# Waits for a burst's loads of q, keys and score rows, moved to the last product of the run in front

## The chip, the cores and the metric

The kernel runs on one core of a Trainium2 chip. The metric is the device time of one execution in microseconds; less is better. The kernel before takes 1772.36 us (median of 3 runs, 1772.31 to 1773.91).

## The reference, cut to what matters

Two attentions over one input x of 2048 rows and 512 columns, 32 heads of 16 columns each, are mixed row by row by a gate.

```python
def _A_ref(x, wqkv, wo):              # side A: full softmax attention over 2048 keys
    scores = jnp.einsum("bhqd,bhkd->bhqk", q, k) * scale
    p = _softmax(scores, axis=-1)
    o = jnp.einsum("bhqk,bhkd->bhqd", p, v)
    return o.transpose(0, 2, 1, 3).reshape(B, S, D) @ wo
...
for s in range(N):                    # side B: 4 segments of 512 rows, causal inside a segment
    logits = jnp.einsum("bhqd,bhkd->bhqk", qs, ks) * scale + mask
    a_dot = jnp.einsum("bhqk,bhkd->bhqd", _softmax(logits, axis=-1), vs)
    a_mem = num / den                 # from M and z, summed over the segments before
    outs.append(g * a_mem + (1.0 - g) * a_dot)
...
return g * a + (1 - g) * b            # g = sigmoid(x . gate_w), one number a row
```

## The kernel before, in words

**Preparation.** The first 300 us or so project x to q, k and v for both sides. q and k are split in a rounded part and a remainder, so that products of rounded operands come out exact enough, and are stored in DRAM. Then come the attention units: a unit is one side, a group of four heads and a chunk of 512 queries. There are 32 units of A and 32 of B, taken in turn. This stage lasts nearly to the end.

**Slots.** A unit of A has 64 slots, one of B has 10. A slot n does two things that belong to different units:

- the score product of the unit that is being computed (`score_part`, line 748): a block of 128 keys against 512 queries of one head, line 763, into one of three PSUM banks `st`; ScalarE then takes its exponential into `p` (line 786, for some slots of B line 783) and so frees the bank;
- the maximum product of a unit 96 slots later (`max_part`, line 226, `LEAD = 96`): 128 queries against 512 keys, line 205, into one of four banks `sm`; VectorE then takes the maximum over the keys (line 238 for A, 253 for B) and so frees the bank. The maxima are transposed (line 196), copied (line 199) and written by a DMA as two further rows of the q tile (line 202), where the score product reads them, so that the exponent is already reduced by the maximum.

Both products use only 48 or 50 rows of the array. Heads 0 and 1 use the lower half of the rows, heads 2 and 3 the upper half, and the order is such that a score product and a maximum product that follow one another use different halves.

**Bursts and runs.** Three slots follow one another (`BURST = 3`); after each third slot the main loop issues a run of other products (lines 1053 to 1073): P @ V of finished blocks (`some_values`, lines 820 and 821), or, while `shared` has any, three products of a late tile of q (line 703) or of the output (line 932). A P @ V step is four products of 17 columns each, one a head, at four positions of the columns of the array (heads at 0, 32, 64, 96); it handles 128 to 512 queries, and a run has one to three such steps. Its operands are plain float32, which the trace shows as two matmuls a product. In the last 94 slots (`wide`) a run comes after each sixth slot.

**Order and queues.** The order on each engine is that in which the program issues (the schedule is manual). Every transfer in question is issued on SyncE's queue. q and keys are loaded some 20 slots ahead of their first maximum product (`PRE = 20`, `loads`, line 282): `load_q` (line 147) issues two transfers for each half of the rows, `load_k` (line 157) two for each half and each chunk of 512 keys. Keys have eight buffers on side A and two on side B. The framework puts a wait for a transfer on the first instruction of an engine that reads what it brought; once an engine has waited for a transfer, its later instructions don't wait again. So a maximum product that is the first to read a new q tile or key chunk waits for the transfers of its half, and a score product that is the first to read the two score rows waits for those. In the program as compiled an instruction carries one wait; further ones stand on semaphore instructions in front of it, one or two on each. They have the line of the product that they stand in front of. The maximum product's own place is taken by the wait for VectorE (its bank), the score product's by the wait for ScalarE.

Of the kernel before, what the change touches and what calls it, by code (L numbers as in the profile page):

```python
# [34 lines left out]
LEAD = 96  # L35
BURST = 3
# [11 lines left out]
def gated_mix(ctx, tc, x, xT, wqkv, a_wo, b_wq, b_wk, b_wv, b_wo, beta, gate_w, out):  # L48
    nc = tc.nc
# [53 lines left out]
    slots = [(u, j) for u in units for j in range(SLOTS[u[0]])]  # L103
# [6 lines left out]
    nS = len(slots)  # L110
# [3 lines left out]
    maxs = []  # L114
    for k in range(NU):
# [3 lines left out]
        start, apart = (33, (3, 3)) if k == 1 else (6, (9, 3)) if k < NU - 1 else (23, (3, 3))  # L119
# [3 lines left out]
        for m in range(len(maxs), len(maxs) + 64 + 10 * len(bs)):  # L123
            r = (m + 1) % 2
# [10 lines left out]
    qt, kt_ = {}, {}  # L135

    def raw(t):

        return t[:].bitcast(F32)
# [4 lines left out]
            "B": [kp.tile([128, 2, CH], F32R, name=f"kB{i}") for i in range(NKB)]}  # L144
    knext = {"A": 0, "B": 0}

    def load_q(u):
        side, g, c = u
        t = qp.tile([128, 2, CH], F32R, tag="q", name=f"q{side}{g}{c}")
        src = qd[side, g // 2, c]  # L150
        for r in range(2):
            hs = slice(4 * (g % 2) + 2 * r, 4 * (g % 2) + 2 * r + 2)
            nc.sync.dma_start(raw(t)[64 * r:64 * r + 16], src[0:16, hs])
            nc.sync.dma_start(raw(t)[64 * r + 16:64 * r + 48], src[:, hs])
        qt[u] = t

    def load_k(u, kc):

        side, g, c = u
        t = kbuf[side][knext[side] % len(kbuf[side])]  # L160
        knext[side] += 1
        src = kd[side, g // 2, kc]
        for r in range(2):
            hs = slice(4 * (g % 2) + 2 * r, 4 * (g % 2) + 2 * r + 2)
            nc.sync.dma_start(raw(t)[64 * r:64 * r + 32], src[:, hs])
            nc.sync.dma_start(raw(t)[64 * r + 32:64 * r + 48], src[0:16, hs])
        kt_[u, kc] = t

    def rows(t, h, n):
# [21 lines left out]
    def transpose_max(us, pool, tag):  # L191

        w = 32 * len(us)
        pt = pool.tile([128, CH], F32, tag=tag, name="mt_ps")
        for i, (_, u, ms) in enumerate(us):
            nc.tensor.matmul(pt[32 * i:32 * i + 32, :128], ms.rearrange("p r a h s -> p (r a h s)").bitcast(F32), identf,  # L196
                             start=True, stop=True, tile_position=(0, 32 * i))
        mt = mp.tile([64, 128], F32R, tag="mt", name="mt")
        nc.scalar.copy(mt[:w], pt[:w, :128])  # L199
        for i, (_, u, ms) in enumerate(us):  # L200
            for r in range(2):
                nc.sync.dma_start(raw(qt[u])[64 * r + 48:64 * r + 50], raw(mt)[32 * i + 16 * r:32 * i + 16 * r + 16])

    def max_product(ps, u, h, s, n0, n, k, k0=0):
        nc.tensor.matmul(ps[:, n0:n0 + n], rows(qt[u][:, :, s * 128:(s + 1) * 128], h, 48), rows(k[:, :, k0:k0 + n], h, 48),  # L205
# [439 lines left out]
    ops = o_ps.tile([128, CH], F32, name="ops")  # L645

    halved = {}
# [28 lines left out]
    def later_tile(c, o):  # L676

        def done():
            full = fr.tile([128, CH], F32, tag="part", name="full")
            nc.scalar.copy(full, ops)  # L680
            t = fr.tile([128, 2, 2, 2, 128], F32R, tag="blk", name="qhalves", bufs=2)
            t = t.rearrange("p a o h t -> p a (o h t)")
            nc.gpsimd.tensor_copy(t[:, 0], full)
            nc.gpsimd.tensor_sub(t[:, 1], full, t[:, 0].bitcast(F32))
            for i in range(2):
                at(n + 12, lambda i=i: nc.sync.dma_start(
                    qd["A", o, c][16 * i:16 * i + 16].rearrange("d h t -> (d h) t"), raw(t[:, i])))


            if o == NO - 1 and c == LATER[0]:  # L690
                for i in range(2):
                    load_halves(("x", LATER[1]), "B", x_later(LATER[1]), (2 * i, 2 * i + 1), n + 2 + 18 * i,
                                [n + 24 + 29 * i, n + 28 + 29 * i])
            elif o == NO - 1:
                for i, (side, w) in enumerate((("A", a_wo), ("B", b_wo))):
                    load_halves(side, side, w, (0, 1), n + 2 + 18 * i, [n + 22 + 8 * i, n + 26 + 8 * i])
                    for k in range(2, 4):
                        load_halves(side, side, w, (k,), n + 50 + 22 * i + 3 * (k - 2), [n + 62 + 18 * i + 5 * (k - 2)])

        def f(i):  # L700
            k, (a, b) = i // 3, ((1, 0), (0, 1), (0, 0))[i % 3]
            assert {("q", k), (("x", c), k)} <= ready
            nc.tensor.matmul(ops, halved["q"][:, k, a, o * 128:(o + 1) * 128], halved["x", c][:, k, b],  # L703
                             start=(i == 0), stop=(i == 11))
            if i == 11:
                done()
        for i in range(12):
            yield lambda i=i: f(i)
# [89 lines left out]
    def some_values(n, most):  # L798

        taken = len(queue)  # L800
        while queue and most and queue[0][0] <= n:
            _, u, i = queue.pop(0)
            most -= 1
            side, g, c = u
            w = 1
            while (queue and most and queue[0][0] <= n and queue[0][1] == u and (i + w) // 4 == i // 4
                   and (side == "A" or PIECES[i + w][0] == PIECES[i][0])):
                queue.pop(0)
                most -= 1
                w += 1  # L810
            p = pt_[u, i // 4]
            if side == "A":
                c0 = q0 = 128 * (i % 4)
                v = vt[u][:, i // 16, i // 4 % 4]
            else:
                b, c0, q0 = PIECES[i]
                v = vt[u][:, b]
            done = i + w == SLOTS[side]
            for h in range(4):
                nc.tensor.matmul(ops[32 * h:32 * h + 17, q0:q0 + 128 * w], v[:, 17 * h:17 * h + 17], p[:, h, c0:c0 + 128 * w],  # L820
                                 start=(i == 0), stop=done, tile_position=(0, 32 * h))
            if done:
                raw = ob.tile([128, CH], F32, tag="o", name="oraw")
                from_bank(n)(raw, ops)
                nc.sync.dma_start(od[side, c][4 * g:4 * g + 4].rearrange("h r t -> (h r) t"), raw)
                stored.add(u)
                if side == "B" and c and g % 2 == 0:
                    octet("M", g // 2, c, n + 4)
                if (side, g ^ 1, c) in stored and u != ("A", NG - 1, NCH - 1):
                    octet(side, g // 2, c, n + (20 if side == "B" and (g < 5 or c < last) else 8))  # L830
                if u in between:
                    shared.extend(output(*between[u]))
                if side == "A" and c == 0:
                    shared.extend(later_tile(LATER[g // NO], g % NO))
                break
        return taken - len(queue)
# [91 lines left out]
    def products(ps, t, b, side, o, start, stop):  # L928

        assert (side, o) in ready  # L930
        for i, (x, w) in enumerate(((1, 0), (0, 1), (0, 0))):
            yield lambda i=i, x=x, w=w: nc.tensor.matmul(ps, t[:, b, x], halved[side][:, o, w], start=start and i == 0,  # L932
                                                         stop=stop and i == 2)

    def out_rows(c, b):
# [104 lines left out]
    n = 0  # L1040
    while n < nS or queue or beside or filled[0] < len(fill):
        for f in beside.pop(n, []):
            f()
        if n < nS:
            score_part(n)
        m = n + LEAD
        if m < nS:
            loads(m + PRE)

            b = oldest()  # L1050
            max_part(m, lambda: banks[b], b)
        run_todo(m)
        if n >= nS or n % (2 * BURST if n in wide else BURST) == (2 * BURST if n in wide else BURST) - 1:
            taken = 0
            if shared:
                for _ in range(3):
                    shared.pop(0)()
            else:
                taken = some_values(n, 8 if n >= nS or n in wide else most(n))
            if n < 5:  # L1060


                for i in range(4):
                    nc.tensor.matmul(ops[:, 128 * i:128 * i + 128], identf, identf, start=True, stop=True)
            if any(e[0] < m + 1 for e in late):
                run_late(st_ps, "st", m + 1)
            else:

                for _ in range(0 if n >= nS and queue else 4 if n not in wide else 11 - taken if taken < 8 else 0):
                    if filled[0] == len(fill) or fill[filled[0]][0] > n:  # L1070
                        break
                    fill[filled[0]][1]()
                    filled[0] += 1
        n += 1
    octet("A", NO - 1, last, None, vector=True)
    assert len(stored) == len(units)
# [43 lines left out]
```

## Time and profile before

| | us |
|---|---|
| runs: median, lowest, highest | 1772.36, 1772.31, 1773.91 |
| the profiled execution: its time | 1773.54 |
| its span, first to last instruction | 1771.8 |
| TensorE busy (matmuls) | 1764.5 |
| VectorE busy | 1568.3 |
| ScalarE busy | 1435.0 |
| GpSimd busy | 641.1 |

The profile is that of one execution. In its rows PE stands for TensorE's matmuls, PEld for its weight loads, DVE for VectorE, ACT for ScalarE, POOL for GpSimd, SP for SyncE. An engine's name with a q is its sequencer: instructions that wait, branch or issue. A group of instructions is written as line, engine, operation, out<-in by the program's names, shape and count, then busy time in us, mean length of one in ns, idle time of the engine before them and what ended it. A row of the timeline has the start (us from the start of the span), the length, the group, and in brackets the idle time before it with what ended it; rows of one kind that overlap or follow closely are merged, with their count. A row of waits has who waited for whom, the sum in us, the count and the longest. Matmuls are pipelined and their ends are modelled, so starts say more than ends. The granted TensorE clock was 1.00 throughout.

### The profile page before, as it was taken

To read this page: it belongs to the slowest core of one execution; us is meant where nothing else is said; L and a number is where in the kernel's file an instruction comes from. 1 tells how busy PE (TensorE), PEld (TensorE's weight loads), DVE (VectorE), ACT (ScalarE), POOL (GpSimd) and SP (SyncE) were. 2 spreads that over 40 slices of the span, in tenths; PEclk is the share of its full clock that TensorE was granted. 3 is DMA by queue.
4 is the path that set the end of the run, shared out by engine and by line. 5 is a ranking of instruction groups with operands and counts; after the bars stand their busy time and mean duration, and the time that the engine had idled before them with its cause. 6 is when DMAs were issued, how large, how long until landed. Compare 5 with 4: busy or idle time off the path is not lost.

```text
span 1771.8 us, 40530 instructions
## 1 busy us (share of the span) xinstructions
PE 1764.5 (100%) x14873; PEld 910.4 (51%) x14873; DVE 1568.3 (89%) x3331; ACT 1435.0 (81%) x2752; POOL 641.1 (36%) x748
## 2 busy tenths in 40 slices
PE   9999999999999999999999999999999999999999
PEld 8887776544444444444444444444444444444444
DVE  4235777999999999999999999999999999999931
ACT  5455444888888888888888888888888888888884
POOL 3002222405161416443434343343434253435343
PEclk9999999999999999999999999999999999999999
DMA  7677556444463436554454545454635454544552
GB/s 247 215 228 246 184 203 190 125 110 135 115 165 107 141 112 180 146 140 135 132 139 124 146 128 146 129 147 119 156 110 151 120 144 116 150 118 138 139 166 62
DMA packets 141270, 261.55 MB, mean 148 GB/s; under 512 B 36328, under 2 KB 58888, under 8 KB 140560
## 3 DMA queue, kind: packets, MB, share of 16 engines
q1 hardware_dynamic: 139712, 257.55, 50.2%
q8 instruction: 119, 1.95, 0.5%
q0 software_dynamic: 1216, 1.14, 0.3%
q14 instruction: 79, 0.65, 0.1%
q10 hardware_dynamic: 144, 0.26, 0.1%
HBM read 174.39 MB, written 83.25 MB: 145 GB/s over the span
## 4 chain that ended last, share of the span: by engine, by line
PE 96%; DVE 1%; DMA 1%; ACT 1%; POOL 1%; issue 0%; SPq 0%; POOLq 0%; DVEq 0%
PE ops L820 33%; PE st L763 27%; PE sm L205 14%; PE pr L330 10%; PE ops L932 4%; PE ops L703 2%; PE sm L932 2%; PE num L533 1%; POOL mn L397 1%; PE pr L420 1%; PE mps L564 0%; DMA qdB<-q 0%; PE mt_ps L196 0%; DMA raw<-xT 0%; PE sm L763 0%; DVE jk L492 0%
## 5 line engine op out<-in xcount | busy, mean ns | idle before, releaser
L786 ACT ACTIVATE p<-st 128x512 f32<-128x512 f32 x2261 | 1190.7, 601 | 152.0 <-PE sm L205 106.0
L238 DVE TENSOR_REDUCE pm<-sm 128x1 f32<-128x512 f32 x2048 | 1278.6, 683 | 11.3 <-PE sm L205 11.2
L205 PE MATMUL sm<-kA,qA 48*128 48x512 f32 x2048 | 668.9, 426 | 0.2
L763 PE MATMUL st<-qA,kA 50*128 50x512 f32 x2014 | 656.7, 431 | 0.0
L820 PE MATMUL ops<-p,vA 128*17 128x256 f32 (+3 forms) x6360 | 552.3, 445 | 0.0
L763 PEld LDWEIGHTS st<-qA,kA 50*128 50x128 f32 x2014 | 326.7, 185 | 422.0 <-ACT p L786 378.2
L205 PEld LDWEIGHTS sm<-kA,qA 48*128 48x128 f32 x2048 | 338.8, 185 | 12.3 <-issue 4.6
L882 POOL TENSOR_TENSOR rcp<-rec,minus 128x32 f32<-128x32 f32 x43 | 234.2, 5446 | 78.8 <-DMA rec<-dend 73.8
L253 DVE CUSTOM_DVE_ANT_0 rest<-sm,mask 128x128 f32<-128x128 f32 (+3 forms) x512 | 247.0, 482 | 0.4
L820 PEld LDWEIGHTS ops<-p,vA 128*17 128x17 f32 x6360 | 129.1, 96 | 214.6 <-issue 183.4
L767 POOL TENSOR_SCALAR_AFFINE_SELECT p<-p 128x512 f32<-128x512 f32 x128 | 79.4, 636 | 320.1 <-ACT p L786 315.5
L205 PE MATMUL sm<-kB,qB 48*128 48x128 f32 (+3 forms) x512 | 166.1, 384 | 0.0
L763 PE MATMUL st<-qB,kB 50*128 50x512 f32 (+1 forms) x495 | 105.3, 329 | 0.3 <-ACT mt L199 0.3
L400 DVE TENSOR_TENSOR q<-full,q 128x512 fp32r<-128x512 f32 x56 | 38.6, 690 | 75.2 <-ACT q L393 68.8
L763 PEld LDWEIGHTS st<-qB,kB 50*128 50x128 f32 x495 | 68.5, 186 | 62.2 <-ACT p L786 50.5
L820 PE MATMUL ops<-p,vB 128*17 128x128 f32 (+3 forms) x1504 | 87.5, 350 | 0.0
L205 PEld LDWEIGHTS sm<-kB,qB 48*128 48x128 f32 x512 | 79.9, 184 | 0.0
L187 POOL CAST ms<-nm 128x16 fp32r<-128x16 f32 x32 | 6.3, 197 | 198.5 <-DVE nm L183 196.7
L397 POOL TENSOR_SCALAR mn<-full 128x512 f32<-128x512 f32 x24 | 36.4, 1516 | 102.9 <-ACT full L392 82.5
L392 ACT COPY full<-pr 128x512 f32<-128x512 f32 x56 | 32.8, 586 | 41.2 <-PE pr L330 37.7
L187 POOL CAST ms<-pm 128x16 fp32r<-128x16 f32 x32 | 6.3, 196 | 127.8 <-DVE pm L253 127.7
L898 POOL TENSOR_TENSOR v<-v,inv 128x512 f32<-128x512 f32 x31 | 39.9, 1286 | 24.5 <-DMA inv<-rdA 20.7
(198 smaller groups left out, 1616.1 us busy)
## 6 DMA issues: line engine op xcount, KB each, us to landing
kA<-kdA SPq DMA_DIRECT2D x256, 128.0 KB
vA<-vdA SPq DMA_DIRECT2D x31, 544.0 KB
kA<-kdA SPq DMA_DIRECT2D x256, 64.0 KB
kdA<-q SPq DMA_DIRECT2D x32, 256.0 KB
qdB<-q SPq DMA_DIRECT2D x32, 256.0 KB
qA<-qdA SPq DMA_DIRECT2D x64, 128.0 KB
kdB<-q SPq DMA_DIRECT2D x32, 256.0 KB
qB<-qdB SPq DMA_DIRECT2D x64, 128.0 KB
```

Source lines behind the costliest of these rows:

```text
L205: nc.tensor.matmul(ps[:, n0:n0 + n], rows(qt[u][:, :, s * 128:(s + 1) * 128], h, 48), rows(k[:, :, k0:k0 + n], h, 48), start=True, stop=True)
L238: nc.vector.tensor_reduce(pm[:, h, s, kc:kc + 1], ps, axis=AX.X, op=ALU.max)
L253: nc.vector.tensor_tensor_reduce(out=tri["rest"][:, 0:w], in0=ps[:, n0:n0 + w], in1=tri["mask"][:, CH - w:], scale=-1.0, scalar=3.0e38, op ...
L330: nc.tensor.matmul(ps, l(a, k), r(b, k), start=(n == 0), stop=(n == 11))
L397: nc.gpsimd.tensor_scalar_min(ph["mn"], full, 0.0)
L763: nc.tensor.matmul(ps[:, n0:n0 + CH - q0], rows(k[:, :, b * 128:(b + 1) * 128], h, 50), rows(q[:, :, q0:], h, 50), start=True, stop=True)
L767: nc.gpsimd.affine_select(out=x, in_=x, pattern=[[0, 4], [1, 128]], base=0, channel_multiplier=-1, compare_op=ALU.is_ge, fill=0.0)
L786: nc.scalar.activation(p[:, h], ps, AF.Exp, scale=SCALE)
L820: nc.tensor.matmul(ops[32 * h:32 * h + 17, q0:q0 + 128 * w], v[:, 17 * h:17 * h + 17], p[:, h, c0:c0 + 128 * w], start=(i == 0), stop=done ...
L882: eng.tensor_tensor(r, rec, minus, op=ALU.pow)
L898: eng.tensor_mul(k["v"], k["v"], k["inv"])
L932: yield lambda i=i, x=x, w=w: nc.tensor.matmul(ps, t[:, b, x], halved[side][:, o, w], start=start and i == 0, stop=stop and i == 2)
```

## The change

Three kinds of transfers are remembered when they are issued: those of q and of keys for each half of the rows, and that of the score rows for each half. Products of P @ V, of late q tiles and of the output go through a wrapper that remembers the last one issued. After the run behind each third slot, from slot 8 on, `wait_early` collects the transfers that the next burst is the first to read (maximum products of the next three slots, score products of the next three slots) and adds to that last product a dependency on each of them. The products of the burst come later on the same engine, so they carry no wait for these transfers any more. In the last 94 slots the function is called after each sixth slot and still looks three slots ahead. No product, no transfer and no buffer is added, removed or put in another place.

```diff
     knext = {"A": 0, "B": 0}
 
+    lands = {}
+    behind = [None]
+
+    def matmul(*args, **kw):
+
+        behind[0] = nc.tensor.matmul(*args, **kw)
+
+    def wait_early(n):
+
+        loads_ = []
+        for m in range(n + 1 + LEAD, n + 1 + BURST + LEAD):
+            if m < nS:
+                u, (r, i) = maxs[m]
+                loads_ += lands.pop(("q", u, r), []) + lands.pop(("k", u, r, u[2] if u[0] == "B" else i // 8), [])
+        for u, j in slots[n + 1:n + 1 + BURST]:
+            for r in range(2):
+                loads_ += lands.pop(("score", u, r), [])
+        for x in loads_:
+            tc.add_manual_dep(behind[0].ins, x.ins.name, mybir.DependencyInfo(
+                mybir.DependencyClass.Sync, mybir.DependencyReason.DATA), reason="loads of the next burst")
+
     def load_q(u):
...
-            nc.sync.dma_start(raw(t)[64 * r:64 * r + 16], src[0:16, hs])
-            nc.sync.dma_start(raw(t)[64 * r + 16:64 * r + 48], src[:, hs])
+            lands["q", u, r] = [nc.sync.dma_start(raw(t)[64 * r:64 * r + 16], src[0:16, hs]),
+                                nc.sync.dma_start(raw(t)[64 * r + 16:64 * r + 48], src[:, hs])]
...
-            nc.sync.dma_start(raw(t)[64 * r:64 * r + 32], src[:, hs])
-            nc.sync.dma_start(raw(t)[64 * r + 32:64 * r + 48], src[0:16, hs])
+            lands["k", u, r, kc] = [nc.sync.dma_start(raw(t)[64 * r:64 * r + 32], src[:, hs]),
+                                    nc.sync.dma_start(raw(t)[64 * r + 32:64 * r + 48], src[0:16, hs])]
...
-                nc.sync.dma_start(raw(qt[u])[64 * r + 48:64 * r + 50], raw(mt)[32 * i + 16 * r:32 * i + 16 * r + 16])
+                lands["score", u, r] = [nc.sync.dma_start(raw(qt[u])[64 * r + 48:64 * r + 50],
+                                                          raw(mt)[32 * i + 16 * r:32 * i + 16 * r + 16])]
...
-                nc.tensor.matmul(ops[32 * h:32 * h + 17, q0:q0 + 128 * w], v[:, 17 * h:17 * h + 17], p[:, h, c0:c0 + 128 * w],
+                matmul(ops[32 * h:32 * h + 17, q0:q0 + 128 * w], v[:, 17 * h:17 * h + 17], p[:, h, c0:c0 + 128 * w],
                                  start=(i == 0), stop=done, tile_position=(0, 32 * h))
...
                     fill[filled[0]][1]()
                     filled[0] += 1
+            if 5 < n < nS:
+                wait_early(n)
         n += 1
```

The products of lines 703 and 932 go through `matmul` in the same way.

More of the change, by code (lines that the diff above doesn't have):

```diff
@@ L702, in f @@
             assert {("q", k), (("x", c), k)} <= ready
-            nc.tensor.matmul(ops, halved["q"][:, k, a, o * 128:(o + 1) * 128], halved["x", c][:, k, b],
+            matmul(ops, halved["q"][:, k, a, o * 128:(o + 1) * 128], halved["x", c][:, k, b],
                              start=(i == 0), stop=(i == 11))
@@ L931, in products @@
         for i, (x, w) in enumerate(((1, 0), (0, 1), (0, 0))):
-            yield lambda i=i, x=x, w=w: nc.tensor.matmul(ps, t[:, b, x], halved[side][:, o, w], start=start and i == 0,
+            yield lambda i=i, x=x, w=w: matmul(ps, t[:, b, x], halved[side][:, o, w], start=start and i == 0,
                                                          stop=stop and i == 2)
```

## The prediction

> **What bounds the kernel now.** I read the page first (shares, then the chain that ended last), then the busy time by stretch, then single bursts in the timeline. A "burst" is three score products (line 763, `st`) and the products of three maximum slots (line 205, `sm`); a "run" is what follows it on TensorE, P @ V (line 820) or output and late-query products (lines 932, 703).
>
> ```profile
> PE 1764.5 (100%) x14873; PEld 910.4 (51%) x14873; DVE 1568.3 (89%) x3331; ACT 1435.0 (81%) x2752; POOL 641.1 (36%) x748
> PE 96%; DVE 1%; DMA 1%; ACT 1%; POOL 1%; issue 0%; SPq 0%; POOLq 0%; DVEq 0%
> 772.00:908.00 136.00, 136.00 (x1278) 62.41 (x1280) 135.96 (x292) 120.93 (x236) 53.91 (x62) 1.00 0.47 135
> ```
>
> TensorE carries 96% of the chain. In the steady stretch (third row: PE, PEld, DVE, ACT, POOL busy of 136 us, clock 1.00) both TensorE and VectorE look full, so a gain on TensorE has to be tested against VectorE; that comes below. The program repeats itself each 136 us (three pairs of units), so this stretch stands for the others.
>
> Now two neighbouring bursts, TensorE's matmuls first (start, length, line), then its weight loads:
>
> ```profile
> 781.77 0.50 PE L763 MATMUL st<-qA,kA 50*128 50x512 f32 x1
> 782.48 0.46 PE L205 MATMUL sm<-kA,qA 48*128 48x512 f32 x1
> 782.87 1.05 PE L820 MATMUL ops<-p,vA 128*17 128x512 f32 x8
> 783.86 0.49 PE L763 MATMUL st<-qA,kA 50*128 50x512 f32 x1
> 784.43 0.40 PE L205 MATMUL sm<-kA,qA 48*128 48x512 f32 x1
> 784.76 0.52 PE L820 MATMUL ops<-p,vA 128*17 128x384 f32 x4
> ...
> 782.27 0.18 PEld L763 LDWEIGHTS st<-qA,kA 50*128 50x128 f32 x1 [0.20 <-ACT p L786]
> 782.45 0.18 PEld L205 LDWEIGHTS sm<-kA,qA 48*128 48x128 f32 x1
> ...
> L205 PEldq EVENT_SEMAPHORE  x2: 51/51/51, 782.3 to 782.4; - x2
> ...
> 783.97 0.41 PEld L763 LDWEIGHTS st<-qA,kA 50*128 50x128 f32 x2
> 784.20 0.19 PEld L205 LDWEIGHTS sm<-kA,qA 48*128 48x128 f32 x1
> ```
>
> The second burst is the ordinary one: from its first product to its run 784.76 - 783.86 = 0.90 us. The first takes 782.87 - 781.77 = 1.10. In the ordinary burst the third `st` and third `sm` have their weights loaded together and run side by side in the two halves of the rows. In the long one the third `st` loads at 782.27, then come two semaphore instructions (51 ns each, about 0.1 us apart; they carry the waits for the loads of a new key chunk), and only then, 0.18 us behind, the weights of the third `sm`. Its product starts 782.48 - 781.77 = 0.71 into the burst against 784.43 - 783.86 = 0.57, ends alone, and the run starts 0.20 late. The wait costs this although nothing was awaited: each of these instructions is 51 ns long. It costs because TensorE's sequencer stands at the third `st` until ScalarE frees its bank ("0.20 <-ACT p"), and what stands behind that is issued just in time.
>
> **The change, part by part.** It computes nothing else and adds no product. It moves the waits for q, key and score-row loads from the first product of a burst that reads them to the last product of the run in front. Removed from the path: the late bursts. The other four in this stretch, first product and run:
>
> ```profile
> 793.01 0.50 PE L763 MATMUL st<-qA,kA 50*128 50x512 f32 x1
> 794.00 0.84 PE L820 MATMUL ops<-p,vA 128*17 128x384 f32 x8
> ...
> 816.70 0.50 PE L763 MATMUL st<-qA,kA 50*128 50x512 f32 x1
> 817.70 0.74 PE L820 MATMUL ops<-p,vA 128*17 128x128 f32 x12
> ...
> 827.51 0.50 PE L763 MATMUL st<-qA,kA 50*128 50x512 f32 x1
> 828.62 0.62 PE L820 MATMUL ops<-p,vA 128*17 128x512 f32 x4
> ...
> 838.70 0.49 PE L763 MATMUL st<-qA,kA 50*128 50x512 f32 x1
> 839.69 0.52 PE L820 MATMUL ops<-p,vA 128*17 128x384 f32 x4
> ```
>
> They take 0.99, 1.00, 1.11 and 0.99. Less 0.91 (the median of the 369 bursts of the same six products without such a wait; the ordinary one above is among them) the five lose 0.19 + 0.08 + 0.09 + 0.20 + 0.08 = 0.64 us in 136 us. The other bursts with such waits lose nothing: there the semaphore instructions stand in front of the first `sm` or come while the run before is still going on. Fifty bursts are late in this way; the first and the last, with their runs:
>
> ```profile
> 373.95 0.50 PE L763 MATMUL st<-qA,kA 50*128 50x512 f32 x1
> 375.05 0.62 PE L820 MATMUL ops<-p,vA 128*17 128x512 f32 x4
> ...
> 1643.29 0.50 PE L763 MATMUL st<-qA,kA 50*128 50x512 f32 x1
> 1644.39 0.62 PE L820 MATMUL ops<-p,vA 128*17 128x512 f32 x4
> ```
>
> Added up over the fifty: **6.1 us**, which is the upper end of the gain. The lower end is nothing, if ScalarE's late bank, not the semaphore instruction, holds these bursts. I stay near the upper end: ScalarE delays the third `st`, whose weights come 0.50 into the burst instead of about 0.34, but a product that starts at 0.57 does not need them sooner; I leave 0.01 to 0.02 us a burst, 0.6 us in all, for it.
>
> What the moved wait costs at the new place. Behind it on TensorE's queue stand the fourth head's product and the whole next burst. It costs nothing where the sequencer is far enough ahead. Rows that show how far: semaphore instructions that already stand right behind a run, and that run's start.
>
> ```profile
> L763 PEldq EVENT_SEMAPHORE  x2: 51/51/51, 523.4 to 524.0; - x2
> 523.77 1.05 PE L820 MATMUL ops<-p,vA 128*17 128x512 f32 x8
> ...
> L196 PEldq EVENT_SEMAPHORE  x1: 51/51/51, 562.5 to 562.5; - x1
> 562.25 0.84 PE L820 MATMUL ops<-p,vA 128*17 128x128 f32 x16
> ...
> L763 PEldq EVENT_SEMAPHORE  x2: 51/51/51, 710.6 to 711.3; - x2
> 711.09 0.97 PE L932 MATMUL ops<-wB,blk 128*128 128x512 f32 x3
> ...
> L820 PE MATMUL ops<-p,vA 128*17 128x256 f32 x1504 | 109.3, 382 | 0.0
> ```
>
> Behind a run of one set of four heads the sequencer has issued everything 0.35 us before the run starts, behind an output run 0.5 before. Behind two sets (562.25, the second set 256 wide) it is done some 0.22 after the start; the run's 16 matmuls end 0.84 in and the last is 0.38 long, so it starts 0.46 in, 0.24 later. Two semaphore instructions put the next weight load off by 0.18 (782.27 to 782.45), so I reckon 0.09 for one and 0.36 for four. By the loops' order some 310 runs get such a wait: 127 of one set of heads, 73 of output or late-query products, 110 of two or more sets. The first two kinds have 0.7 us or more before the last product: nothing. In the third kind two instructions fit, barely; ten runs whose second set is 128 wide may miss by 0.1. Bounds: 0, and 110 x 0.18 = 20 us if there is no cover at all. I take 0.5 us, since the rows lie on the covered side.
>
> Does a load land later than the earlier wait? The list of waits has no row in which TensorE waits for a DMA in the steady stage. The tightest key load, its issue and its first reader, and a transfer with a landing time:
>
> ```profile
> L166 SPq DMA_DIRECT2D kB<-kdB x2: 420/906/1393, 688.8 to 690.7; - x2
> L205 PE MATMUL sm<-kB,qB x2: 324/355/386, 697.2 to 697.4; 48*128 48x128 f32 x1, 48*128 48x384 f32 x1
> vA<-vdA POOLq DMA_DIRECT2D x1, 544.0 KB, 4.1
> ```
>
> Issued 6.5 us ahead (697.2 - 690.7); 4.1, for eight times the bytes on GpSimd's queue, leaves 2.4, and the wait moves up by 0.5 to 1.4 us. Nothing. SyncE's queue is untouched: no transfer is moved, and its own waits are as before. The score rows of the last two units, after 1700 us, are sent nearer to their use; a stop there falls on two runs at most, an estimated 1 us each, and is in the range.
>
> **VectorE.** Its rows:
>
> ```profile
> L238 DVE TENSOR_REDUCE pm<-sm 128x1 f32<-128x512 f32 x1344 | 838.2, 683 | 0.0
> L253 DVE CUSTOM_DVE_ANT_0 rest<-sm,mask 128x128 f32<-128x128 f32 (+2 forms) x337 | 162.8, 483 | 0.3
> 784.45 3.07 DVE L238 TENSOR_REDUCE pm<-sm 128x1 f32<-128x512 f32 x5
> PEld sm L205 <- DVE pm L238: 3.3, 11, 0.4
> ```
>
> Busy time flatters: five reductions in 3.07 us are (3.07 - 0.68) / 4 = 0.598 apart though each is 0.683 long, so each covers 0.085 of the next. What VectorE needs in the 952 us from 636 to 1588 is 1344 x 0.598 + 337 x (0.483 - 0.076) = 941 us, 98.9%. It has 11 us of slack there, about 15 in the whole stage, against a gain of 6. And TensorE waits for VectorE's banks 3.3 us in the whole run. So VectorE is next late, but not yet. For moments in which TensorE gets ahead of it and waits for a bank I take off 0.3 us.
>
> Sum: 6.1 - 0.6 - 0.5 - 0.3 = 4.7 us. The profiled execution would go from 1773.54 to 1768.8 (its span from 1771.8 to 1767.1); it was itself among the slow end of the runs shown (1772.31 to 1773.91, median 1772.36). From the median: **1767.7 us**, its own range 1765.9 to 1769.4. About 0.2% (3.5 us) is what a measurement of this kernel can tell from no change, so this lies not far beyond it.
>
> The Trainium skill speaks against the change in one place: "TensorE: Matmul & The Clock Gate", section "Architectural detail: the array is 16× 32×32, not 1× 128×128", says TensorE has a queue of 64 and pulls weight loads ahead of matmuls in flight. By that rule a satisfied wait inside a burst would be hidden and nothing gained (the first rival's time). The trace disagrees at 782.45, where the weights come 0.18 us after those of the partner product, behind the two semaphore instructions.
>
> **Rivals.** (1) No change, 1772.4 us (1771.5 to 1773): ScalarE's bank or VectorE sets the pace, and what the bursts save is waited for elsewhere. For it: the 0.20 us wait for ScalarE at 782.27, and VectorE at 98.9%. Against: the gap of 0.18 between the two weight loads holds the semaphore instructions and no wait for an engine; VectorE's 11 us.
>
> (2) Slower, about 1776.5 us: the waits cut into the runs. The place is the fourth head's product of runs with two sets; the price 0.09 to 0.36 us a run at most; with 0.08 for each of the 110 runs, 8.8 us against the 4.7. It decides from the point where the sequencer reaches that product less than 0.18 us (0.36 with eight loads) before it is to start. For it: only 0.24 at 562.5, with everything of the burst queued behind. Against: that row is read behind the last product, and the new place is two products earlier.
>
> (3) That the change doesn't do what it says: a run without any product would leave the waits at an older one; then they move further up, where loads had 2.4 us, and the time is the forecast's.
>
> **How the numbers follow.** Forecast, (3) in it: 0.66, of which 0.06 lies within 0.2%. Rival 1: 0.20. Rival 2: 0.14, of which 0.02 within 0.2%. Faster 0.60, same 0.28, slower 0.12. The range goes from 1765.4 (all 6.1 us and a little) to 1772.9, which takes in the forecast and most of rival 1 and leaves rival 2 out.
>
> **What would show it.** Right: the semaphore instructions of line 205 are gone from the steady stage, and about as many stand at lines 820, 932 and 703; the five bursts of each 136 us take 0.91 to 0.93; runs keep their length (0.98 for one set 512 wide); VectorE's reductions stay 0.598 apart more evenly. Wrong: runs of two sets longer by about 0.1; late bursts unchanged at 1.1 with the third `st` still waiting for ScalarE; or new waits of line 205 for VectorE of several us.

## The result, and the profile after

The changed kernel takes **1768.99 us** (median of 17 runs, 1767.84 to 1770.38), the kernel before 1773.05 on the same chip (17 runs, 1772.1 to 1773.91): 4.06 us less, a ratio of 0.9978 with a 95% interval of 0.9971 to 0.9984. The forecast was 1767.7, from a median of before that was 0.7 lower; as a difference it said 4.7 us. The profiled execution of the changed kernel has a span of 1767.5 us, that of before 1771.8.

First the page of the changed kernel: TensorE's busy time with its neighbours, and the engines' shares of the chain that ended last.

```profile
PE 1760.7 (100%) x14873; PEld 908.9 (51%) x14873; DVE 1564.4 (89%) x3331; ACT 1436.3 (81%) x2752; POOL 641.0 (36%) x748
...
PE 96%; DVE 1%; ACT 1%; DMA 1%; POOL 1%; issue 0%; SPq 0%; POOLq 0%; ACTq 0%
```

TensorE holds 96% of the chain as before, with as many matmuls. So the 4 us must lie in how closely its products follow one another. This is the burst that the prediction looked at first (781.77 in the kernel before), from the timeline of the changed kernel, products first, then weight loads.

```profile
780.32 0.50 PE L785 MATMUL st<-qA,kA 50*128 50x512 f32 x1
...
780.90 0.42 PE L227 MATMUL sm<-kA,qA 48*128 48x512 f32 x1
781.25 1.05 PE L152 MATMUL ops<-p,vA 128*17 128x512 f32 x8
...
780.82 0.18 PEld L785 LDWEIGHTS st<-qA,kA 50*128 50x128 f32 x1 [0.20 <-ACT p L808]
780.82 0.18 PEld L227 LDWEIGHTS sm<-kA,qA 48*128 48x128 f32 x1
```

The third score product (`st`, now line 785) still waits 0.20 us for ScalarE. But the third maximum product (`sm`, now line 227) loads its weights in the same moment, 780.82, where it was 0.18 later before, and the run (all products of runs now have the wrapper's line, 152) starts 781.25 - 780.32 = 0.93 after the burst's first product in place of 1.10. The semaphore instructions stand where the change puts them, as the view of line 152 shows, for this stretch and for the whole run, beside line 227.

```profile
L152 PEldq EVENT_SEMAPHORE  x2: 51/51/51, 780.8 to 780.9; - x2
L152 PEldq EVENT_SEMAPHORE  x542: 51/51/51, 315.6 to 1713.9; - x181
L227 PEldq EVENT_SEMAPHORE  x22: 51/51/51, 160.5 to 306.4; - x22
```

The kernel before, its line 205:

```profile
L205 PEldq EVENT_SEMAPHORE  x447: 51/51/51, 160.7 to 1682.1; - x149
```

Their times are those of issue: 780.8 to 780.9, 0.35 us and more before the run that they belong to starts at 781.25. They are as long as ever, 51 ns; they now fall where TensorE has work in hand. The other four late bursts of the same stretch, in the same order:

```profile
791.33 0.50 PE L785 MATMUL st<-qA,kA 50*128 50x512 f32 x1
792.26 0.84 PE L152 MATMUL ops<-p,vA 128*17 128x384 f32 x8
...
815.08 0.49 PE L785 MATMUL st<-qA,kA 50*128 50x512 f32 x1
815.63 0.18 PEld L785 LDWEIGHTS st<-qA,kA 50*128 50x128 f32 x1 [0.25 <-ACT p L808]
815.63 0.18 PEld L227 LDWEIGHTS sm<-kA,qA 48*128 48x128 f32 x1
816.05 0.74 PE L152 MATMUL ops<-p,vA 128*17 128x128 f32 x12
...
825.87 0.50 PE L785 MATMUL st<-qA,kA 50*128 50x512 f32 x1
826.80 1.05 PE L152 MATMUL ops<-p,vA 128*17 128x512 f32 x8
...
836.87 0.49 PE L785 MATMUL st<-qA,kA 50*128 50x512 f32 x1
837.80 0.84 PE L152 MATMUL ops<-p,vA 128*17 128x384 f32 x8
```

They take 0.93, 0.97, 0.93 and 0.93 us. Before they took 0.99, 1.00, 1.11 and 0.99. Three are mended. The one at 815.08 (816.70 before) is not: its third score product and its third maximum product load together at 815.63, and still it takes 0.97: ScalarE frees the bank only 0.55 into the burst. They loaded together before the change as well, so that the wait in that burst had nothing to hold up. The kernel before:

```profile
817.26 0.18 PEld L763 LDWEIGHTS st<-qA,kA 50*128 50x128 f32 x1 [0.23 <-ACT p L786]
817.27 0.18 PEld L205 LDWEIGHTS sm<-kA,qA 48*128 48x128 f32 x1
```

**Where the 4 us are.** I set the two traces side by side, burst by burst: 774 bursts, each cut in a front (first product to the start of the run) and a run (from there to the next burst). The sums of the differences, after less before:

| | bursts | us |
|---|---|---|
| late bursts that are mended (fronts) | 39 | -4.72 |
| late bursts that are not (816.70 and its kind, one in each 136 us) | 10 | -0.01 |
| bursts behind the runs that grow, see below | 10 | -0.88 |
| those runs | 10 | +0.87 |
| bursts that now wait for VectorE | 15 | +1.06 |
| all else, none over 0.05 | | -0.34 |
| together | 774 | -4.02 |

The third pair of weight loads tells the first two rows apart. In the 39 bursts that are mended, the third `sm` loads 0.07 to 0.21 us behind the third `st` before, and at most 0.02 behind it after. In the ten that are not, it loads within 0.004 us of it in both kernels, but the third `st` itself comes 0.54 to 0.56 into the burst, where in the 39 it comes 0.48 to 0.50 into it.

Another 0.26 us of the spans' difference lies ahead of the first burst (303.12 against 302.86 us), where both kernels have the same instructions.

### The profile page after: what moved, and what is told of

It reads as the page before. It is cut to its first block, busy times and chain, and to the rows that moved or that the text cites. A ratio compares the mean times of both kernels' runs of the same rounds, so it can differ in the third digit from the quotient of the medians.

```text
span 1767.5 us, 40472 instructions
## 1 busy us (share of the span) xinstructions
PE 1760.7 (100%) x14873; PEld 908.9 (51%) x14873; DVE 1564.4 (89%) x3331; ACT 1436.3 (81%) x2752; POOL 641.0 (36%) x748
## 4 chain that ended last, share of the span: by engine, by line
PE 96%; DVE 1%; ACT 1%; DMA 1%; POOL 1%; issue 0%; SPq 0%; POOLq 0%; ACTq 0%
PE ops L152 40%; PE st L785 27%; PE sm L227 14%; PE pr L352 10%; PE sm L152 2%; PE num L555 1%; POOL mn L419 1%; PE pr L442 1%; PE mps L586 0%; DMA qdB<-q 0%; PE mt_ps L217 0%; DMA raw<-xT 0%; PE sm L785 0%; DVE jk L514 0%; ACT ex L426 0%; DVE pm L260 0%
```

## The experiments

Theory: a wait instruction costs where it stands, not that it is there. Behind a score product that waits for ScalarE until just then, it makes the maximum product behind it late; anywhere else the sequencer is ahead and it is free. What is won that way is taken back in part by VectorE. Rivals: what counts is the number of instructions, or the lateness of the loads; or what is given back has nothing to do with VectorE. The first four kernels ran on one chip (before: 1773.18, 33 runs), the next four on another (1773.10, 21 runs), the last two on a third (1773.91, 10 runs). All edits are to the changed kernel, except where it is said.

| kernel | median (lowest to highest) | ratio to before, 95% interval |
|---|---|---|
| e1_first_score | 1769.11 (1768.1 to 1769.58) | 0.9976, 0.9967 to 0.9985 |
| e2_first_of_run | 1772.58 (1770.4 to 1774.7) | 0.9997, 0.9989 to 1.0006 |
| e3_third_slot | 1769.33 (1768.36 to 1770.82) | 0.9979, 0.997 to 0.9988 |
| e4_first_two | 1773.18 (1772.09 to 1773.69) | 0.9999, 0.999 to 1.0008 |
| e5_before_448 | 1770.01 (1768.85 to 1771.32) | 0.998, 0.9971 to 0.9989 |
| e6_after_448 | 1765.98 (1764.24 to 1767.82) | 0.9959, 0.9946 to 0.9973 |
| e7_third_max | 1785.29 (1784.55 to 1785.46) | 1.0068, 1.0055 to 1.0081 |
| e8_first_not_wide | 1769.44 (1768.82 to 1770.38) | 0.9981, 0.9972 to 0.9989 |
| e9_before_384 | 1768.44 (1767.7 to 1769.34) | 0.9971, 0.996 to 0.9982 |
| e10_after_384 | 1762.85 (1762.58 to 1763.87) | 0.9939, 0.9926 to 0.9953 |

### Which waits: the third slot's alone, or the others alone

```diff
# e3_third_slot
-        for m in range(n + 1 + LEAD, n + 1 + BURST + LEAD):
+        for m in range(n + BURST + LEAD, n + 1 + BURST + LEAD):
-        for u, j in slots[n + 1:n + 1 + BURST]:
+        for u, j in slots[n + BURST:n + 1 + BURST]:
# e4_first_two
+        for m in range(n + 1 + LEAD, n + BURST + LEAD):
+        for u, j in slots[n + 1:n + BURST]:
```

> Only the waits of the third slot of a burst are moved to the run, about half of all (264 of some 510 semaphore instructions); those of the first and second slot stay. Theory: of the 5.7 us the third slot's have 4.5 to 5 (all late bursts but the ten with a wait in the second slot alone), the ten longer runs don't come, VectorE takes back about 0.8: 3.7 to 4.2 us under before. Rival A (all waits cost alike): half of the gain, 2 us under before.

> Only the waits of the first and second slot are moved, the third slot's stay in the burst. Theory: at most the ten bursts with a wait in the second slot alone are mended (-0.7) and a part of the others with waits in both (-0.3 to -0.8), the ten longer runs come (+0.8): within 1 us of the kernel before. Rival A (all waits cost alike): half of the gain, 2 us under before.

Moving only the third slot's waits gives 3.85 us, within the noise the whole change; moving only those of the first and second slot gives nothing. One thing came otherwise than expected: the ten runs that grow (the table above has them) are there in e3 too (0.83 us in sum), and not only in e4 (0.81). The waits of either part are enough to lengthen them.

### Where they go: the first score product of the burst

```diff
# score_part, behind the first score product of a burst; the call behind the run is taken out
+            if n > 8 and n % BURST == 0 and n not in waited:
+                waited.add(n)
+                behind[0] = x
+                wait_early(n - 1)
```

> The waits stand at the first score product of the burst that reads the loads, instead of the last product of the run in front of it. Theory (a semaphore instruction costs only where the sequencer has just been held by a wait for ScalarE or VectorE; right behind a run it is ahead): the late bursts are mended as in the changed kernel (-5.7 us) and no run grows (0 instead of +0.8), VectorE still takes back about 1.0: 4.7 us under the kernel before, 0.6 to 0.7 under the changed kernel's 4.06. Rival A (each wait inside a burst costs some 13 ns, 310 of them make the 4 us): the waits are in the burst again, so no gain, within 1 us of the kernel before. Rival B (only the place at a product of the run helps): likewise no gain.

It is 4.07 us under the kernel before, as good as the change, with none of the moved waits in a run: no run grows, and the 39 mended fronts gain 5.00. But it is no better, where 0.6 us more was expected. The ten runs that grow in the changed kernel show why. Before, one of them and what follows it:

```profile
761.12 0.84 PE L820 MATMUL ops<-p,vB 128*17 128x384 f32 x8
761.89 0.50 PE L763 MATMUL st<-qA,kA 50*128 50x512 f32 x1
...
762.93 0.30 PE L820 MATMUL ops<-p,vB 128*17 128x128 f32 x4
```

The same in the changed kernel, with the semaphore instructions of that run (view of line 152):

```profile
759.68 0.92 PE L152 MATMUL ops<-p,vB 128*17 128x384 f32 x8
760.53 0.50 PE L785 MATMUL st<-qA,kA 50*128 50x512 f32 x1
...
761.48 0.30 PE L152 MATMUL ops<-p,vB 128*17 128x128 f32 x4
...
L152 PEldq EVENT_SEMAPHORE  x2: 51/51/51, 759.6 to 759.7; - x2
```

The run took 761.89 - 761.12 = 0.77 and takes 760.53 - 759.68 = 0.85: its first product is itself issued just in time (the first of the two semaphore instructions is a wait for ScalarE in front of it, and the run starts some 0.1 later), so the added wait puts the fourth head's product off. But the next burst took 762.93 - 761.89 = 1.04 and now takes 0.95. Its later score products wait for ScalarE; whether TensorE arrives early or late, they start when the bank is free. e1 takes the 0.08 out of the run, and the next burst is 1.04 again.

### The first product of the run

```diff
# e2_first_of_run: behind[0] = None ahead of each run, and in the wrapper
-        behind[0] = nc.tensor.matmul(*args, **kw)
+        x = nc.tensor.matmul(*args, **kw)
+        if behind[0] is None:
+            behind[0] = x
# e8_first_not_wide: the last product again in the last stage
+        if behind[0] is None or n in wide:
```

> The waits stand at the first product of the run in front instead of its last. Theory: in the ten runs that grew by 0.08 us the semaphore instructions came behind a wait for ScalarE at the run's first product; now they come before that wait and are done while it is awaited, so the +0.8 us goes; late bursts mended (-5.7), VectorE takes back 1.0: 4.7 us under before. In runs whose burst ended just in time four semaphore instructions (0.36 us) may show: up to 0.5 us back. Rival (the place in the run makes no difference, the ten runs grew for another reason): 4.06 us under before, with the ten runs still 0.85 long.

It missed: 0.6 us under before in place of 4.7, with times that spread over 4.3 us where those of e1 spread over 1.5. The trace, that of its slowest run, has one stop that the others don't have, in the last stage (timeline, TensorE's products):

```profile
1702.77 0.50 PE L787 MATMUL sm<-qB,kB 50*128 50x128 f32 x5
1705.12 1.56 PE L152 MATMUL ops<-p,vA 128*17 128x512 f32 x8 [1.85 <-DMA qB<-mt]
```

The run waits 1.85 us for the score rows of one of the last units: the run lasts 2.8 us there, its first product comes that much ahead of the next burst, and the rows had not landed. And it costs twice. The stretches around the stop (length, then PE, PEld, DVE, ACT, POOL busy, granted clock, DMA):

```profile
1703.00:1705.00 2.00, 0.28 (x4) 0.07 (x2) 0.00 (x0) 2.00 (x5) 0.65 (x1) 1.00 0.03 8
1705.00:1706.00 1.00, 0.88 (x8) 0.16 (x8) 0.00 (x0) 0.34 (x1) 0.59 (x2) 0.76 0.06 16
1706.00:1707.00 1.00, 1.00 (x5) 0.38 (x2) 0.21 (x1) 0.00 (x0) 0.64 (x2) 0.50 1.03 139
1707.00:1708.00 1.00, 1.00 (x3) 0.78 (x3) 0.48 (x1) 0.00 (x0) 0.00 (x0) 0.50 0.83 213
1708.00:1709.00 1.00, 1.00 (x4) 0.74 (x3) 0.00 (x0) 0.00 (x0) 0.00 (x0) 0.53 0.99 381
1709.00:1710.00 1.00, 1.00 (x9) 0.64 (x9) 0.00 (x0) 0.00 (x0) 0.00 (x0) 1.00 1.10 393
```

The granted clock falls to 0.50 for 3.4 us by these rows, right behind the stop. Burst by burst the front loses 1.92 us for the wait and the run behind it, in which the clock is low, 1.57: together 3.5 us of the 4.1 that the change is worth; no other run of e2 differs from that of before by 0.05. e8 was to say whether that single stop is all:

> The variant with the waits at the first product of the run, but in the last stage (the wide one, from slot 2258 or so) at the last product as in the changed kernel. Theory (the other variant lost 3.5 us in a single stop in that stage, on score rows that hadn't landed): 1769.0, 4 us under before, and no stop at 1705. Rival (waits ahead of a run hold up the run everywhere): within 1 us of the 1772.6 of that variant.

It is 1769.44, and in its timeline the same run starts without a stop:

```profile
1701.51 1.05 PE L152 MATMUL ops<-p,vA 128*17 128x512 f32 x8
```

So in front of a run (e8), at its last product (the change) or behind it (e1), the waits cost nothing that these times show, as long as the load has landed.

### The worst place

```diff
# e7_third_max, in max_part; the call behind the run is taken out
-            max_product(ps, u, h, s, 0, CH, kt_[u, kc])
+            behind[0] = max_product(ps, u, h, s, 0, CH, kt_[u, kc])
+            if 8 < m - LEAD < nS - 1 and (m - LEAD) % BURST == BURST - 1:
+                wait_early(m - LEAD)
```

> The same waits, at the worst place that the theory knows: all waits for the loads of a burst stand at the maximum product of the third slot of the burst in front of it, so behind the third score product, which waits for ScalarE. They fall a whole burst earlier than in the kernel before, so that no transfer is late. By the compiled program 156 bursts then hold two or more of them there and 115 one, where the kernel before has 20 with two, all late by 0.175 us, and some 90 with one, of which some 20 were late by 0.066. Theory (a wait instruction costs where it stands behind a score product that is released just then): slower than before by 8 to 25 us, 1781 to 1798; the two-wait bursts late by 0.1 to 0.18 each. Rival (their number costs, or loads that land late): no more than the kernel before, 1769 to 1773.

It is 12.2 us slower than before, 16 slower than the changed kernel, with the same waits a whole run earlier. Against the changed kernel, burst by burst: of 87 bursts of six products with two such instructions 58 are late, by 0.18 us in the mean; all 20 with four are late, by 0.20; of 64 with one, 30, by 0.06. In bursts of seven products, 48 of 49 with two lose nothing. One of the late ones, its weight loads and then the semaphore instructions in the view of line 227:

```profile
789.99 0.18 PEld L789 LDWEIGHTS st<-qA,kA 50*128 50x128 f32 x1 [0.19 <-ACT p L812]
790.22 0.18 PEld L227 LDWEIGHTS sm<-kA,qA 48*128 48x128 f32 x1
790.65 0.35 PEld L152 LDWEIGHTS ops<-p,vA 128*17 128x17 f32 x16 [0.24 <-issue]
...
L227 PEldq EVENT_SEMAPHORE  x2: 51/51/51, 790.0 to 790.1; - x2
```

The picture is that of the kernel before: the third `st` at 789.99, two instructions of 51 ns, the third `sm` at 790.22, the run late. The number of instructions doesn't do this: from the first burst on, the sequencer has 597 semaphore instructions in e7, 594 in e1 and 595 in the changed kernel. Nor does a late load, for these waits are earlier than any. The Trainium skill says in "TensorE: Matmul & The Clock Gate" (section "Architectural detail: the array is 16× 32×32, not 1× 128×128") that weight loads can be pulled ahead of matmuls in flight. If that held across waits too, all of this would cost nothing; the 12.2 us and the weights at 790.22 say that here it doesn't reach past a wait that stands in the queue.

### VectorE

Fifteen bursts got longer by some 0.07 each. The same burst in the two kernels, VectorE's reductions, first product, weight loads of the third `st` (the second of the two in its row) and the third `sm`, and the run. Before:

```profile
854.78 1.28 DVE L238 TENSOR_REDUCE pm<-sm 128x1 f32<-128x512 f32 x2
...
855.11 0.50 PE L763 MATMUL st<-qA,kA 50*128 50x512 f32 x1
...
855.22 0.44 PEld L763 LDWEIGHTS st<-qA,kA 50*128 50x128 f32 x2
...
855.51 0.18 PEld L205 LDWEIGHTS sm<-kA,qA 48*128 48x128 f32 x1
...
856.01 0.41 PE L820 MATMUL ops<-p,vB 128*17 128x128 f32 x8
```

After:

```profile
853.02 1.27 DVE L260 TENSOR_REDUCE pm<-sm 128x1 f32<-128x512 f32 x2
853.21 0.50 PE L785 MATMUL st<-qA,kA 50*128 50x512 f32 x1
...
853.32 0.45 PEld L785 LDWEIGHTS st<-qA,kA 50*128 50x128 f32 x2
...
853.75 0.18 PEld L227 LDWEIGHTS sm<-kA,qA 48*128 48x128 f32 x1
...
854.17 0.41 PE L152 MATMUL ops<-p,vB 128*17 128x128 f32 x8
```

The first of the two reductions takes 0.68 and ends at 855.46 before and at 853.70 after. In both kernels the third `sm` loads 0.05 us later: it waits for that bank. So it is in all fifteen of these bursts, in both kernels: 0.053 or 0.054 us from the end of a reduction to this weight load. But TensorE has come nearer to VectorE: the burst starts 0.33 us behind the start of that reduction before, 0.19 after. The weights come 0.40 and 0.54 into the burst, the run 0.90 and 0.96. No row has a bracket for this wait: the weight loader was busy with the score product's weights meanwhile, so the list of waits goes from 3.3 to 3.6 us only.

```profile
PEld sm L227 <- DVE pm L260: 3.6, 12, 0.4
```

To test it, VectorE's work was made smaller in both kernels. The maximum then leaves out 64 (e5, e6) or 128 (e9, e10) of the 512 keys of a chunk; as the exponent is reduced by the same number for all keys of a row, the softmax keeps its value.

```diff
-            nc.vector.tensor_reduce(pm[:, h, s, kc:kc + 1], ps, axis=AX.X, op=ALU.max)
+            nc.vector.tensor_reduce(pm[:, h, s, kc:kc + 1], ps[:, :448], axis=AX.X, op=ALU.max)
```

e5 and e9 are the kernel before with this, e6 and e10 the changed kernel (448 and 384).

> The kernel before, but VectorE's maxima of the A side are taken over 448 of the 512 keys (64 keys are left out of the maximum, which only shifts the exponent). One reduction then takes about 0.6 us in place of 0.68, and the banks of the maxima come free about 0.08 us earlier. Together with e6. Theory (the fourteen or so bursts that the changed kernel loses, 1.0 us in sum, wait for VectorE): the forty bursts that stand late by their semaphore instructions stay late here, since those wait for no bank; the time is that of the kernel before or up to 4 us less, 1769 to 1773. Rival (VectorE sets the pace everywhere): more than 4 us less, under 1769.

> The changed kernel with the same shorter maxima. Theory: against e5 the forty mended bursts give 4.7 to 5.1 us as before, and no burst behind them grows for VectorE, so that the sum over fronts and runs, burst by burst, falls by 4.7 to 5.2 us where it fell by 4.0; by the times 1764 to 1768, and e6 over e5 0.9970 to 0.9973. Rival (what was given back, 1.0 us, has nothing to do with VectorE): the same 4.0 us, fourteen bursts longer by 0.07 again, e6 over e5 0.9977.

> The kernel before with the maxima of the A side over 384 of the 512 keys (128 keys are left out of the maximum), together with e10: a second step of the pair e5 and e6, whose times stood 4.0 us apart while their bursts, summed front by front and run by run, stood 4.8 us apart (the stage ahead of the first burst took 0.75 us more in the profile of e6, and it takes 302.0 to 304.6 us in the ten profiles so far with the same instructions). The late bursts stay: 1767 to 1770.5.

> The changed kernel with the maxima over 384 keys. Theory (VectorE takes back about 1 us of the gain in the changed kernel): again no burst behind a run grows for VectorE, the bursts' sum falls by 4.7 to 5.2 us against e9 once more, and the times stand 4.8 us apart, 0.9971 to 0.9974. Rival (the difference is the same 4 us with any speed of VectorE, and the grown bursts are paid for elsewhere): a sum of 4.0 and times 4.0 apart, 0.9977.

The groups of VectorE from 374 to 1640 us, in the kernel before, e5 and e9; the last number is the idle time before them:

```profile
L238 DVE TENSOR_REDUCE pm<-sm 128x1 f32<-128x512 f32 x1789 | 1115.6, 683 | 0.0
```

```profile
L238 DVE TENSOR_REDUCE pm<-sm 128x1 f32<-128x448 f32 x1789 | 1022.1, 619 | 37.3 <-PE sm L205 28.2 <-PE st L763 3.2
```

```profile
L238 DVE TENSOR_REDUCE pm<-sm 128x1 f32<-128x384 f32 x1789 | 910.3, 552 | 102.4 <-PE sm L205 90.2 <-PE st L763 8.3
```

| | difference of medians | burst by burst | bursts longer by over 0.035 |
|---|---|---|---|
| 512 keys (after less before) | -4.06 | -4.02 | 15, +1.06 |
| 448 keys (e6 less e5) | -4.03 | -4.82 | 1, +0.05 |
| 384 keys (e10 less e9) | -5.59 | -5.01 | 0 |

With VectorE at leisure the grown bursts are gone, and the change is worth 4.8 to 5.0 us in the traces. The times alone don't settle it: by the first pair they stand 4.03 apart, the rival's number, by the second 5.59, and the five runs of e6 alone spread over 3.6 us. In the profiles of the first pair, 0.75 us of the missing difference lies ahead of the first burst, as e9's expectation says. VectorE also costs the kernel before some microseconds by itself: e5 stands 3.1 us under it, e9 5.5 (in the profiles 2.3 and 3.0 burst by burst, and 1.2 and 2.1 ahead of the first burst, where some maxima are shorter as well), with the late bursts as late as ever (1.10 us for that of 781.77 in e5).

## Why the prediction was right, and where its sizes were off

- **The mechanism** is as forecast: e3, e4 and e7 show that it is the wait's place behind the third score product that costs, and e1 and e8 that other places don't.
- **6.1 us of late bursts** was too much for what the waits cause. One of the five in 136 us, that of 816.70, is late by ScalarE: 0.06 to 0.09 us in each of ten, 0.7 us in sum, of which 0.01 was won. The prediction took its lateness for that of the wait because a semaphore instruction stood in the burst; e3, which leaves that instruction where it was, has the same 0.97 there. The rows to look at were its third pair of weight loads (817.26 and 817.27, together), not the burst's length.
- **ScalarE's bank, 0.6 us:** the mended bursts take 0.93, 0.02 over the ordinary 0.91 and 0.6 us in sum over the 39, which is what was left for it. That it is ScalarE's bank is as argued there; no run separates it. The two points together are 1.3 us of the 6.1, where 0.6 was taken off: the fronts that were mended gave 4.72.
- **Waits at the new place, 0.5 us:** the fear was for runs of two sets. It didn't come: 112 runs of two or more sets got a wait, and none changed by more than 0.002 us. Ten runs did grow, but runs of one set, which were put down at nothing, because their own first product is issued just in time. It cost nothing net (0.87 against 0.88 in the bursts behind), since ScalarE held those anyway. Of the price list, 0.18 for two instructions came out as said; one cost 0.06 in place of 0.09 and four 0.20 in place of 0.36, each in the bursts of e7 that were late.
- **VectorE, 0.3 us:** 1.06 in truth, and this is the step that failed in size. The slack of 11 us was right as a sum (the distances from start to start on VectorE, where it doesn't idle, give the same 941 us of need). But slack over 952 us says nothing on a single burst: the gain comes in pieces of 0.1 to 0.2 us, and behind each piece TensorE runs nearer to VectorE until a burst's third bank isn't free.
- **The sum:** that 4.7 came within 0.7 of 4.06 is in part luck. The late bursts gave 0.8 us less and VectorE took 0.8 more than forecast; against that stand the 0.5 that the moved waits did not cost and 0.3 won in small pieces, for which the forecast had no term.
- **Loads:** no run of the changed kernel stops for one in the steady stage, and none at the end. In the range I had put a stop in the last stage at 1 us; the one of e2 is 3.5, nearly half of it while the clock was low.
- **Rivals:** no change was wrong since e7 and e3 move the time as the theory says; slower failed at its own place, the fourth head's product of runs of two sets. The third, that the change doesn't do what it says, is refuted by the rows of lines 152 and 227 above.

No version stands out above the changed kernel: e1, e3 and e8 are within 0.5 us of it. What is left is VectorE's and ScalarE's share, not that of the waits.

## What to carry to other kernels

A satisfied wait is not free: it is an instruction, here of 51 ns, in order. In this kernel it cost where the engine's sequencer had no lead, that is right behind an instruction that itself waits until the last moment (12.2 us in e7, and nothing in sum at the other places). Look for pairs of instructions that should start together and don't, ask what stands between them in the queue, and put it where the engine has work in hand. And when an engine is near its limit, don't count its slack as a sum: the gain is spent in the bursts where the two engines meet.

## What the runs showed of the hardware that was not expected

- Behind one stop of TensorE of 1.85 us its granted clock was down at 0.50 for 3.4 us (e2, rows above; no other of the twelve profiles shows a drop before its last microsecond). The Trainium skill ("TensorE: Matmul & The Clock Gate", section "HAM oscillation — how this bites in real kernels") describes this for waits for a DMA, but as a matter of gaps of over about 3.4 us; here one of about half of that was followed by it. But the same trace has a stop of 1.75 us ahead of the first burst, behind which the clock stayed at 1.00 (rows below). What tells the two apart, no run shows.

```profile
140.94 0.50 PE L354 MATMUL pr<-xh,wvl 128*128 128x512 f32 x1 [1.75 <-ACT vs L463]
141.00:142.00 1.00, 1.00 (x5) 0.82 (x6) 0.69 (x2) 0.41 (x1) 0.00 (x0) 1.00 0.87 154
```

- Four semaphore instructions behind a late score product cost little more than two: 0.20 against 0.18 us in a burst that is late, one 0.06 (e7).
- A wait that delays a weight load can be absent from the list of waits, when the loader is busy with another load in that time: 1.06 us were lost to VectorE, and the list grew by 0.3.
- The stretch ahead of the first burst takes 302.0 to 304.6 us in the eight profiles in which it holds the same instructions (in e5, e6, e9 and e10, whose maxima are shorter there too, 301.1 to 302.7). A spread of 2.6 us is more than half of the effect; a comparison burst by burst leaves it out.
